# A chunked recurrence and two feed-forward layers on one core: how values are loaded, who copies the keys, and how the first layer's last two blocks are ordered

## The chip, the cores and the metric

The kernel runs on one NeuronCore of a Trainium2 chip. Its engines work side by side, each through its own queue in the order written: TensorE (PE, matmuls; PEld are its weight loads), VectorE (DVE), ScalarE (ACT), GpSimd (POOL), and SyncE (SP), whose queue here issues all DMA transfers to 16 DMA engines. The metric is the device time of one execution, in microseconds.

## The reference

Three steps follow each other. For 4 x 8 heads and 768 steps a state of 40 x 40 is read, decayed and updated; then two feed-forward layers work on 3072 tokens of 320 values, 2048 wide inside.

```python
for t in range(S):
    y[:, :, t] = np.einsum('bhd,bhde->bhe', rt, state)
    Sa = np.einsum('bhde,bhe->bhd', state, at)
    state_decay = state * wt[:, :, None, :] - np.einsum('bhd,bhe->bhde', Sa, bt)
    state = state_decay + np.einsum('bhd,bhe->bhde', vt, kt)
...
h = x @ w_in                                       # layer one
g = np.where(pos, h, np.where(neg, 0.0, (h + beta) ** 2 / (4.0 * beta)))
x = g @ w_out
...
h = x @ w_in                                       # layer two
r = np.maximum(h, 0.0)
g = s * (r * r) + b
return g @ w_out
```

The weights arrive as 64-bit floats.

## The kernel before

**Attention.** The 768 steps are cut into 24 chunks of 32 steps; two chunks make a unit (NU = 12). Per unit, `prep_a` builds running products of the decays, scales keys and a, and forms a triangular matrix, which `inverse` and `mend` invert. Per chunk, `chain_a` carries the state: xp, then up, then sp (the new state, from xr and the keys in kbi), and `chain_b` gives the output: tq (the state turned, copied into kbs), tp (copied into the upper half of vu), gg (from vu and ggr), py (from ggr and kbs). So the keys stand twice in SBUF: in KBI, written by DVE from tk and tb in `keys`, and in KBS, copied from KBI. Values lie in VU, whose lower half is loaded per chunk by `loads_v`, and whose upper half takes tp.

**Layers.** Layer one works on blocks of 256 tokens (12 of them, two chunks each), layer two on blocks of 512 (6). `fin0` and `fin1` make h for two slices or one slice of 128 inner columns, `post` turns h into g and splits it into a high part gh (ACT) and a rest gl (POOL in layer one, DVE in layer two), `fout0` and `fout1` add its product with w_out into acc. Output products run two steps behind the input products (LAG = 2). Every product is made of three, high by high, high by low and low by high, in float32r. `tok_tile` turns a tile of tokens with PE (ptx) and splits it likewise; layer one's input tiles have two slots (xh), so block n takes the slot of block n-2.

**Weights.** Each of 16 slices has two parts (w_in, 384 words a partition, and w_out, 320). `loads_w` brings the 64-bit words, `convert` makes 32-bit floats of them (ACT L233 and L234, DVE L235 and L236, POOL L238: t) and `split` a high part (L326) and the rest (L327). A slice of layer two lies where layer one's slice lay: its load waits until the last block of layer one has used that slice (`fin`, `fout`).

**Order.** The instructions are not put in this order by hand: `Order` is a list scheduler that runs when the program is built. Each function above is a thread that yields operations with planned durations, waits on flags, takes slots and sets its urgency (`Prio`, from START, STEP, TILE and DUE). At each step the engine that can begin earliest takes the most urgent of its operations ready within a small window. Filler matmuls (`warm`, L1022) keep PE busy until the first two input tiles of layer one are there. Planned durations set only the order; on the chip each queue waits for its semaphores.

## Time and profile before

| what | value |
|---|---|
| median of 3 runs | 1259.22 us (1254.14 to 1263.78) |
| the profiled execution | 1254.48 us, its span 1252.7 us |
| PE, PE weight loads | 1127.8 us, 1018.9 us |
| DVE, ACT, POOL | 730.4 us, 738.4 us, 343.4 us |
| mean granted clock of PE | 0.945 |
| DMA, first queue | 164054 packets, 124.69 MB, 40.7% of 16 engines' span |

Busy times overlap, and each is a share of the whole span. The stages differ: the first 150 us fill the pipeline, then attention and layer one share the engines to about 770 us, then layer one goes on alone to 861 us, and layer two takes the rest. The granted clock is 1 at 2.4 GHz and 0.5 at 1.2 GHz; a mean lies between.

### The profile page before, as it was taken

Reading aid. Unit: us, or ns where it says so; the run is one execution under the profiler, and the core shown is the slowest. Engines: PE = TensorE matmul, PEld = TensorE weight load, DVE = VectorE, ACT = ScalarE, POOL = GpSimd, SP = SyncE. Lnnn points to the kernel's source line nnn. Section 1 sums busy time; section 2 is a strip of 40 time slices with the busy share of each in tenths; the row PEclk is TensorE's granted clock in tenths of the full one; section 3 lists DMA queues with packets and bytes.
Section 4 is the critical chain, followed back from the end, with each engine's and each line's share of the span. In section 5 each row is a group of like instructions: output and inputs, shape, how many; then the busy total and the mean of one; then the engine's idle time right before and its main releaser. Section 6 shows DMA issues by size and latency. Waiting matters only on the chain. (4 is left out here: it accounts for less than half of the span.)

```text
span 1252.7 us, 45743 instructions
## 1 busy us (share of the span) xinstructions
PE 1127.8 (90%) x19834; PEld 1018.9 (81%) x19834; DVE 730.4 (58%) x1629; ACT 738.4 (59%) x1521; POOL 343.4 (27%) x299
## 2 busy tenths in 40 slices
PE   4798787898999889897999999998989999999995
PEld 4797776787888778776887899998878989888895
DVE  4777886636866776665786443237974344444432
ACT  2434774465675556655565576779876555555552
POOL 4456572321552323414141112335420000000000
PEclk9898698888999999889898999999989999999998
DMA  7875646545558657565644231129001010101001
GB/s 201 255 213 157 145 89 160 131 99 125 150 110 168 132 128 165 138 154 127 153 97 99 53 99 39 36 66 349 14 1 47 1 47 1 47 7 28 17 6 24
DMA packets 164264, 127.71 MB, mean 102 GB/s; under 512 B 118838, under 2 KB 137398, under 8 KB 162806
## 3 DMA queue, kind: packets, MB, share of 16 engines
q1 hardware_dynamic: 164054, 124.69, 40.7%
q8 instruction: 158, 2.59, 0.9%
q14 instruction: 52, 0.43, 0.1%
HBM read 90.83 MB, written 19.66 MB: 88 GB/s over the span
## 5 line engine op out<-in xcount | busy, mean ns | idle before, releaser
L926 POOL TENSOR_TENSOR gl<-g,gh 128x512 fp32r<-128x512 f32 x96 | 126.1, 1314 | 450.2 <-ACT gh L924 377.7
L946 PE MATMUL h<-xh,w 128*128 128x256 f32 x1152 | 234.5, 306 | 5.1 <-DVE g L914 3.5
L946 PEld LDWEIGHTS h<-xh,w 128*128 128x128 f32 x1152 | 186.4, 202 | 12.3 <-DVE g L914 4.0
L973 PE MATMUL acc<-w,gh 128*128 128x320 f32 x768 | 187.4, 330 | 2.0 <-issue 2.0
L991 PE MATMUL acc<-w,gh 128*128 128x320 f32 x768 | 174.6, 314 | 1.2 <-DVE o L1002 0.8
L924 ACT CAST gh<-g 128x512 fp32r<-128x512 f32 x192 | 118.8, 619 | 70.9 <-DVE g L914 40.8
L991 PEld LDWEIGHTS acc<-w,gh 128*128 128x128 f32 x768 | 133.6, 191 | 10.4 <-ACT o L1004 1.5
L926 DVE TENSOR_TENSOR gl<-g,gh 128x512 fp32r<-128x512 f32 x96 | 71.6, 746 | 116.1 <-ACT gh L924 114.4
L973 PEld LDWEIGHTS acc<-w,gh 128*128 128x128 f32 x768 | 127.2, 193 | 7.9 <-issue 1.7
L973 PE MATMUL acc<-w,gl 128*128 128x320 f32 x384 | 120.8, 315 | 1.8 <-issue 1.6
L914 DVE SCALAR_TENSOR_TENSOR g<-h,g 128x512 f32<-128x512 f32 x96 | 65.9, 686 | 96.2 <-ACT h L913 84.0
L991 PE MATMUL acc<-w,gl 128*128 128x320 f32 x384 | 120.1, 313 | 1.8 <-DVE gl L926 1.7
L946 PE MATMUL h<-xl,w 128*128 128x256 f32 x384 | 113.2, 295 | 3.0 <-issue 3.0
L920 ACT ACTIVATE g<-g,sbt 128x512 f32<-128x512 f32 x96 | 78.4, 817 | 60.3 <-DVE g L918 60.2
L911 ACT ACTIVATE g<-h,sbt 128x512 f32<-128x512 f32 x96 | 66.0, 688 | 64.8 <-PE h L946 59.2
L918 DVE SCALAR_TENSOR_TENSOR g<-h,g 128x512 f32<-128x512 f32 x96 | 66.3, 690 | 61.8 <-ACT g L917 61.7
L917 ACT ACTIVATE g<-h 128x512 f32<-128x512 f32 x96 | 57.4, 598 | 71.2 <-PE h L956 71.2
L1022 PE MATMUL h<-w 128*128 128x256 f32 x616 | 84.6, 299 | 16.4 <-ACT w L326 16.4
L1022 PEld LDWEIGHTS h<-w 128*128 128x128 f32 x616 | 80.6, 205 | 17.7 <-ACT w L326 16.4
L238 POOL TENSOR_TENSOR t<-t,w 128x384 int32<-128x384 int32 x64 | 68.0, 1070 | 92.2 <-DVE t L236 74.0
L956 PE MATMUL h<-xx,w 128*128 128x512 f32 x288 | 77.9, 405 | 4.6 <-ACT w L326 2.8
L946 PEld LDWEIGHTS h<-xl,w 128*128 128x128 f32 x384 | 77.8, 203 | 3.3 <-issue 3.2
(103 smaller groups left out, 2192.8 us busy)
## 6 DMA issues: line engine op xcount, KB each, us to landing
w<-in_w_in SPq DMA_DIRECT2D x32, 384.0 KB
w<-in_w_out SPq DMA_DIRECT2D x32, 320.0 KB
ekb<-in_kb_em SPq DMA_DIRECT2D x12, 832.0 KB
vu<-in_v_em SPq DMA_DIRECT2D x24, 416.0 KB
ggr<-in_r_em SPq DMA_DIRECT2D x24, 416.0 KB
kbs<-kbi SPq DMA_DIRECT2D x48, 160.0 KB
tk<-ekb SPq DMA_DIRECT2D x48, 128.0 KB
suf<-in_ws_em SPq DMA_DIRECT2D x12, 429.0 KB
```

What stands on the lines that cost most here:

```text
L238: (pool, n, lambda: nc.gpsimd.tensor_tensor(out=t, in0=t, in1=lo, op=ALU.add)),
L911: yield act(512, lambda: nc.scalar.activation(out=g, in_=h, func=AF.Relu, bias=sbt[:, 2:3]), more=93)
L914: yield dve(512, lambda: nc.vector.scalar_tensor_tensor(out=g, in0=h, scalar=1.0, in1=g, op0=ALU.subtract, op1=ALU.add))
L918: yield dve(512, lambda: nc.vector.scalar_tensor_tensor(out=g, in0=h, scalar=0.0, in1=g, op0=ALU.max, op1=ALU.mult))
L920: yield act(512, lambda: nc.scalar.activation(out=g, in_=g, func=AF.Identity, scale=sbt[:, 0:1], bias=sbt[:, 1:2]), more=230)
L924: yield act(512, lambda: nc.scalar.copy(out=gh, in_=g))
L926: yield mk(512, lambda: eng.tensor_tensor(out=gl, in0=g, in1=gh.bitcast(F32), op=ALU.subtract))
L946: yield pe(8 * 118, lambda: [nc.tensor.matmul(h[:, i, :], lhsT=a, rhs=b, start=m == 0, stop=m == 7) for m, (a, b) in enumerate(mm)])
L956: yield pe(4 * 224, lambda: [nc.tensor.matmul(h, lhsT=a, rhs=b, start=4 * i + m == 0, stop=4 * i + m == 7) for m, (a, b) in enumerate(mm[4 ...
L973: yield pe(6 * 147, lambda: [nc.tensor.matmul(acc[0, n][u], lhsT=a, rhs=b, start=p == 0 and m == 0, stop=p == NFF // 2 - 1 and m == 5) for ...
L991: yield pe(3 * 147, lambda: [nc.tensor.matmul(acc[1, n][u], lhsT=a, rhs=b, start=f == 0 and m == 0, stop=f == NFF - 1 and m == 2) for m, ( ...
L1022: yield pe(2 * 109, lambda: [nc.tensor.matmul(h[:, i, :], lhsT=wh[:, 0:128], rhs=wh[:, 0:256], start=True, stop=True) for i in range(2)], ...
```

## The change

Four edits. The values of a chunk are loaded without the zeros of the upper half, as two DMAs of 40 partitions with runs of 128 B instead of one of 104 partitions with rows of 4096 B; VU is cleared once by POOL. KBS gets its second copy of the keys from two ACT copies instead of two DMAs. In layer one, blocks 10 and 11 are worked off together, slice by slice, and begin when both have their input; block 11's accumulators take the slots of py and a. In layer two, the high part of the weights is made by POOL (a cast, `tensor_copy`) instead of ACT, and loads and conversions of its weights are due one unit earlier.

```diff
@@ -309,7 +309,7 @@
         yield Op("POOL", 500, lambda: nc.gpsimd.memset(LN, 0.0))
         yield pool(1, lambda: nc.gpsimd.memset(ones, 1.0))
         yield pool(1, lambda: nc.gpsimd.memset(tot, 0.0))
-        for i, t in enumerate(XA + XR + [KBS]):
+        for i, t in enumerate(XA + [VU] + XR + [KBS]):
             yield Op("POOL", 890, lambda t=t: nc.gpsimd.memset(t, 0.0))
             if i < 4:
                 od.set("clearx", i + 1)
@@ -321,9 +321,12 @@
     def hold(f, part, dtype):
         return wts.tile([128, 2 * (DM if part else 384)], dtype, tag=f"w{f}_{part}", name="w")
 
-    def split(w, t, n, mk, eng):
+    def split(l, w, t, n, mk, eng):
         wh, wl = w[:, 0:n], w[:, n:2 * n]
-        yield act(n, lambda: nc.scalar.copy(out=wh, in_=t.bitcast(F32)))
+        if l:
+            yield pool(n, lambda: nc.gpsimd.tensor_copy(out=wh, in_=t.bitcast(F32)), rate=1.2)
+        else:
+            yield act(n, lambda: nc.scalar.copy(out=wh, in_=t.bitcast(F32)))
         yield mk(n, lambda: eng.tensor_tensor(out=wl, in0=t.bitcast(F32), in1=wh.bitcast(F32), op=ALU.subtract))
 
     raw = [{}, {}]
@@ -331,10 +334,10 @@
     def loads_w(l):
 
         for f in range(NFF):
-            yield Prio(START + DUE["weights"] + TILE * f - 30 + (STEP * (NU - 1) + 60) * l)
+            yield Prio(START + DUE["weights"] + TILE * f - 30 + (STEP * (NU - 2) + 60) * l)
             for part in range(2):
                 if l:
-                    yield Wait(("fout" if part else "fin", (NBLK - 1) * NFF // 2 + f // 2 + 1))
+                    yield Wait(("fout" if part else "fin", (NBLK - 1) * NFF // 2 + f // 2 + 1), (("xr0", NC)))
                 elif f:
                     yield Wait((f"cl0{part}", f))
                 n = DM if part else 384
@@ -346,7 +349,7 @@
 
         n = DM if part else 384
         for f in range(odd, NFF, 2):
-            yield Prio(START + DUE["weights"] + TILE * f + (STEP * (NU - 1) + 60) * l)
+            yield Prio(START + DUE["weights"] + TILE * f + (STEP * (NU - 2) + 60) * l)
             yield Wait((f"cl{l}{part}", f + 1))
             w = raw[l].pop((f, part))
             yield Acq(f"t{part}")
@@ -354,7 +357,7 @@
             for mk, size, op in f64_ops(nc, w.rearrange("p (n x) -> p n x", x=2), t, n):
                 yield mk(size, op)
             w = hold(f, part, F32R)
-            yield from split(w, t, n, *((dve2, nc.vector) if l else (pool, nc.gpsimd)))
+            yield from split(l, w, t, n, *((dve2, nc.vector) if l else (pool, nc.gpsimd)))
             wtile[l][f, part] = (w[:, 0:n], w[:, n:2 * n])
             od.set(f"w{l}{part},{f}")
             od.rel(f"t{part}")
@@ -656,7 +659,9 @@
             if i:
                 od.rel("tk")
             yield Wait(("Y", c))
-            yield dma(128 * 2560, lambda: [nc.sync.dma_start(out=KBS[r0:r0 + 64, x], in_=KBI[r0:r0 + 64, x]) for x, r0 in ((0, 64), (1, 0))], 2, ("kbs", c + 1), 650)
+            for x, r0 in ((0, 64), (1, 0)):
+                yield act(640, lambda: nc.scalar.copy(out=KBS[r0:r0 + 64, x], in_=KBI[r0:r0 + 64, x]), x > 0)
+            od.set("kbs", c + 1)
 
     def decays():
         for c in range(NC):
@@ -679,8 +684,9 @@
     def loads_v():
         for c in range(NC):
             yield due("chain", c / 2)
-            yield Wait(("lk", 1), ("G", c))
-            yield dma(104 * 4096, lambda: nc.sync.dma_start(out=VU.rearrange("p a x t -> p (a x t)"), in_=v_em[c]), 1, ("ldv", c + 1))
+            yield Wait(("clear", 1), ("G", c))
+            yield dma(80 * 2048, lambda: [nc.sync.dma_start(out=VU[64 * x:64 * x + 40, :, 0, :], in_=v_em[c, x].rearrange("e (p t) -> e p t", t=C))
+                                          for x in range(2)], 2, ("ldv", c + 1))
 
     def loads_r():
         for c in range(NC):
@@ -964,16 +970,20 @@
     def fout0(n, p):
         yield Wait((f"g0,{n},{p}", 1), (f"w01,{2 * p}", 1), (f"w01,{2 * p + 1}", 1))
         gh, gl = gs.pop((0, n, p))
+        where = ("py", "a") if n == NBLK - 1 else ("o0", "o1")
         if p == 0:
-            for u in range(2):
-                yield Acq(f"o{u}")
-            acc[0, n] = [po.tile([128, DM], F32, tag=f"o{u}", name="acc") for u in range(2)]
+            for slot in where:
+                yield Acq(slot)
+            if n == NBLK - 1:
+                acc[0, n] = [pa.tile([128, DM], F32, tag="y", name="acc", bufs=1), pa.tile([128, DM], F32, tag="a", name="acc")]
+            else:
+                acc[0, n] = [po.tile([128, DM], F32, tag=f"o{u}", name="acc") for u in range(2)]
         for u in range(2):
             mm = [x for i in range(2) for x in g_products(0, gh, gl, 2 * p + i, 256 * i + 128 * u)]
             yield pe(6 * 147, lambda: [nc.tensor.matmul(acc[0, n][u], lhsT=a, rhs=b, start=p == 0 and m == 0, stop=p == NFF // 2 - 1 and m == 5)
                                        for m, (a, b) in enumerate(mm)])
             if p == NFF // 2 - 1:
-                od.spawn(finish(0, n, u, f"o{u}"), due("moe", n).value)
+                od.spawn(finish(0, n, u, where[u]), due("moe", n).value)
         od.rel("gh")
         od.set("fout", n * NFF // 2 + p + 1)
 
@@ -1026,20 +1036,21 @@
         late = []
         yield Wait(("const", 1))
         for l in range(2):
-            for n in range(NBLK // 2 if l else NBLK):
-                yield due("moe", 2 * n + NU if l else n)
-                yield Wait((f"xr{l}", 4 * n + 4 if l else 2 * n + 2))
+            for ns in [(n,) for n in range(NBLK // 2)] if l else [(n,) for n in range(NBLK - 2)] + [(NBLK - 2, NBLK - 1)]:
+                yield due("moe", 2 * ns[0] + NU if l else ns[0])
+                yield Wait((f"xr{l}", 4 * ns[0] + 4 if l else 2 * ns[-1] + 2))
                 steps = NFF if l else NFF // 2
                 for p in range(steps):
-                    yield from (fin1 if l else fin0)(n, p)
-                    late.append((fout1 if l else fout0, n, p))
-                    if p == steps - 1:
-                        for slot in (("tk", "tk", "ew") if n % 2 else ("ekb", "es")) if l else ("xh",):
-                            od.rel(slot)
-                        od.set(f"blk{l}", n + 1)
-                    if len(late) > LAG:
-                        fout, *at = late.pop(0)
-                        yield from fout(*at)
+                    for n in ns:
+                        yield from (fin1 if l else fin0)(n, p)
+                        late.append((fout1 if l else fout0, n, p))
+                        if p == steps - 1:
+                            for slot in (("tk", "tk", "ew") if n % 2 else ("ekb", "es")) if l else ("xh",):
+                                od.rel(slot)
+                            od.set(f"blk{l}", n + 1)
+                        if len(late) > LAG:
+                            fout, *at = late.pop(0)
+                            yield from fout(*at)
         for fout, *at in late:
             yield from fout(*at)
 
@@ -1185,7 +1196,7 @@
     d["ws_em"], d["wp_em"] = units(e[..., 1:]), units(e[..., :C])
     d["kb_em"] = units(np.stack([emaj(x["k"]), emaj(x["b"])], axis=2))
     d["a_em"] = np.ascontiguousarray(x["a"].reshape(NP, 2, NC, C, D).transpose(2, 1, 4, 0, 3)).reshape(NC, 2, D, NP * C)
-    d["v_em"] = emaj(x["v"], 0, 0, C).reshape(NC, 104, -1)
+    d["v_em"] = np.ascontiguousarray(x["v"].reshape(NP, 2, NC, C, D).transpose(2, 1, 4, 0, 3)).reshape(NC, 2, D, NP * C)
     e = emaj(x["r"])
     d["r_em"] = np.zeros((NC, 104, 2, NP, C), f)
     d["r_em"][:, 0:40, 0], d["r_em"][:, 64:104, 1] = e[:, 0:40], e[:, 64:104]
```

What this does to the order, at three places. Line numbers of the new file are 3 to 11 higher from the second edit on.

First, SP's queue in the attention stage. Before, one stretch of it:

```order
L569 DMA lscr_172<-ln 64x512 x2
L683 DMA vu<-in_v_em 104x1024
L587 DMA lt<-lscr_172 128x8x32
L406 DMA ekb<-in_kb_em 104x2048
L477 DMA ascr_161<-am 128x8x32
L659 DMA kbs<-kbi 64x640 x2
L689 DMA ggr<-in_r_em 104x1024
L400 DMA pre<-in_wp_em 104x1024
```

After, the same stretch:

```order
L572 DMA lscr_172<-ln 64x512 x2
L480 DMA ascr_161<-am 128x8x32
L590 DMA lt<-lscr_172 128x8x32
L480 DMA ascr_161<-am 128x8x32
L409 DMA ekb<-in_kb_em 104x2048
L556 DMA la<-ascr_161 64x16x16 x2
L403 DMA pre<-in_wp_em 104x1024
```

And ACT's queue after, at one chunk of that stage (xr, kbs, x and gh are written here):

```order
L917 ACTIVATE g<-h,sbt 128x512
L918 ACTIVATE h<-g,sbt 128x512
L919 ACTIVATE h<-h 128x512
L729 COPY xr_103<-up 32x320 x3
L663 COPY kbs<-kbi 64x640 x2
L729 COPY xr_103<-up 32x320
L930 CAST gh<-g 128x512
L790 COPY kbs<-tq 40x320 x2
L897 COPY x<-x 128x64
```

The loads of kbs are gone from SP, and two copies to kbs stand on ACT, here between the third and the last copy to xr.

Second, PE's queue where block 10 begins (acc are block 9's output products, ptx turns an input tile, h the next input products). Before:

```order
L973 MATMUL acc<-w,gh 128x320 x2
L973 MATMUL acc<-w,gl 128x320
L973 MATMUL acc<-w,gh 128x320 x2
L973 MATMUL acc<-w,gl 128x320
L865 MATMUL ptx<-ident,x 128x128 x3
L973 MATMUL acc<-w,gh 128x320 x2
L973 MATMUL acc<-w,gl 128x320
L973 MATMUL acc<-w,gh 128x320 x2
L973 MATMUL acc<-w,gl 128x320
L946 MATMUL h<-xh,w 128x256
L946 MATMUL h<-xl,w 128x256
```

After:

```order
L983 MATMUL acc<-w,gh 128x320 x2
L983 MATMUL acc<-w,gl 128x320
L983 MATMUL acc<-w,gh 128x320 x2
L983 MATMUL acc<-w,gl 128x320
L871 MATMUL ptx<-ident,x 128x128 x3
L983 MATMUL acc<-w,gh 128x320 x2
L983 MATMUL acc<-w,gl 128x320
L983 MATMUL acc<-w,gh 128x320 x2
L983 MATMUL acc<-w,gl 128x320
L871 MATMUL ptx<-ident,x 128x128 x3
L952 MATMUL h<-xh,w 128x256
L952 MATMUL h<-xl,w 128x256
```

Both times the ptx turns tiles of block 11, whose slot block 9 has just given back. Before, block 10's h needs none of them, and its own input lies ready. After, the first h belongs to the pair, for which both tiles must be split, and the second ptx stands directly ahead of it.

Third, DVE's queue where layer two's first gl stands (g and gl are the blocks' activations, t and w the weights' conversion). Before:

```order
L236 SCALAR_TENSOR_TENSOR t<-w,t 128x320
L236 SCALAR_TENSOR_TENSOR t<-w,t 128x384
L918 SCALAR_TENSOR_TENSOR g<-h,g 128x512
L871 TENSOR_TENSOR xl<-ptx,xh 128x2x128
L872 TENSOR_TENSOR xd<-ptx,xd 64x128
L918 SCALAR_TENSOR_TENSOR g<-h,g 128x512
L926 TENSOR_TENSOR gl<-g,gh 128x512
L327 TENSOR_TENSOR w<-t,w 128x320
L327 TENSOR_TENSOR w<-t,w 128x384
L327 TENSOR_TENSOR w<-t,w 128x320
L327 TENSOR_TENSOR w<-t,w 128x384
L926 TENSOR_TENSOR gl<-g,gh 128x512
```

After:

```order
L920 SCALAR_TENSOR_TENSOR g<-h,g 128x512
L330 TENSOR_TENSOR w<-t,w 128x384
L924 SCALAR_TENSOR_TENSOR g<-h,g 128x512
L1012 COPY o<-acc 128x320
L330 TENSOR_TENSOR w<-t,w 128x320
L330 TENSOR_TENSOR w<-t,w 128x384
L932 TENSOR_TENSOR gl<-g,gh 128x512
L236 SCALAR_TENSOR_TENSOR t<-w,t 128x320
L924 SCALAR_TENSOR_TENSOR g<-h,g 128x512
L235 TENSOR_SCALAR t<-w 128x384
L235 TENSOR_SCALAR t<-w 128x320
L235 TENSOR_SCALAR t<-w 128x384
```

Before, four subtractions (w<-t,w) follow the first gl; after, three stand ahead of it. In the whole queue, 9 of the 32 L235, 9 of the 32 L236 and 5 of the 32 subtractions stood ahead of that gl before, and 14, 13 and 13 now.

## Rows read from the trace of the kernel before

**Rows 1.** By stage: from:to, length, busy PE PEld DVE ACT POOL, PE clock, DMA share, GB/s.

```profile
150.00:765.90 615.90, 550.28 (x14799) 488.85 (x14793) 397.16 (x1020) 367.69 (x820) 195.96 (x160) 0.93 0.55 122
765.90:799.80 33.90, 33.90 (x423) 33.07 (x420) 9.13 (x21) 23.91 (x45) 10.32 (x8) 1.00 0.14 40
799.80:861.30 61.50, 61.50 (x475) 61.24 (x473) 25.73 (x52) 50.55 (x101) 25.35 (x21) 1.00 0.42 141
861.30:938.30 77.00, 67.28 (x326) 57.46 (x325) 67.74 (x116) 62.55 (x133) 30.39 (x29) 0.91 0.21 75
938.30:997.40 59.10, 59.10 (x334) 53.25 (x333) 25.72 (x42) 34.69 (x59) 0.00 (x0) 1.00 0.10 25
```

**Rows 2.** PE's waits, 150 to 766 us: total us, times, longest.

```profile
PE pq L607 <- issue: 11.3, 7, 4.6
PE tq L762 <- issue: 10.2, 4, 5.2
...
PE sp L741 <- ACT vu L802: 1.3, 2, 0.8
...
PE pl L596 <- issue: 0.7, 1, 0.7
```

**Rows 3.** PE in order of time near 708 us: start, length, group.

```profile
707.75 0.57 PE L607 MATMUL pq<-pn,en 32*16 32x16 f32 x50
709.52 0.27 PE L607 MATMUL pq<-pn,en 32*16 32x16 f32 x14 [1.21 <-issue]
```

**Rows 4.** Busy time in the first and last of seven long gaps.

```profile
209.49:214.74 5.25, 0.00 (x1) 0.00 (x0) 3.54 (x12) 0.32 (x1) 0.69 (x1) 0.85 0.88 202
...
617.39:620.35 2.96, 0.00 (x1) 0.03 (x1) 0.11 (x1) 0.06 (x1) 0.00 (x0) 0.84 0.91 202
```

**Rows 5.** PE's waits, 861 to 939 us.

```profile
PE ptx L865 <- DMA x<-x2scr: 2.4, 1, 2.4
```

**Rows 6.** Busy time while one load of vu, of aa, two of kbs move.

```profile
747.00:749.60 2.60, 2.60 (x79) 2.43 (x78) 1.58 (x4) 1.75 (x5) 0.00 (x0) 1.00 0.66 170
690.50:691.60 1.10, 1.01 (x29) 0.71 (x27) 1.05 (x4) 0.45 (x1) 0.00 (x0) 1.00 0.77 119
241.90:244.60 2.70, 0.95 (x77) 0.81 (x80) 2.51 (x14) 1.01 (x3) 0.00 (x0) 0.87 0.70 138
```

**Rows 7.** Instructions by line: a GpSimd memset.

```profile
L313 POOL MEMSET kbs<- 128x1280 f32 x1 | 1.2, 1170 | 0.0
```

**Rows 8.** SP's queue, waits ahead of the kbs loads.

```profile
SPq L659 <- PE py L832: 30.8, 16, 12.1
...
SPq L659 <- PE ptx L865: 19.9, 3, 18.5
```

**Rows 9.** Instructions by line: two ACT copies of other sizes.

```profile
L784 ACT COPY kbs<-tq 40x320 f32<-40x320 f32 x92 | 38.6, 420 | 27.0 <-PE tq L762 25.9
...
L499 ACT ACTIVATE tk<-suf 104x1024 f32<-104x1024 f32 x12 | 12.7, 1061 | 0.2
```

**Rows 10.** PE in order of time near 146 us.

```profile
146.31 0.87 PE L865 MATMUL ptx<-ident,x 128*128 128x128 f32 x3 [4.84 <-DVE x L884]
```

**Rows 11.** Instructions by line, 836 to 936 us: conversions and their neighbours.

```profile
L238 POOL TENSOR_TENSOR t<-t,w 128x384 int32<-128x384 int32 (+1 forms) x32 | 33.6, 1058 | 42.9 <-DVE t L236 24.9 <-ACT g L920 5.4 <-DVE t L235 3.5
...
L236 DVE SCALAR_TENSOR_TENSOR t<-w,t 128x384 int32<-128x384 int32 (+1 forms) x32 | 21.0, 671 | 0.2
...
L327 DVE TENSOR_TENSOR w<-t,w 128x384 fp32r<-128x384 f32 (+1 forms) x32 | 18.4, 597 | 1.9 <-ACT w L326 1.8
...
L926 DVE TENSOR_TENSOR gl<-g,gh 128x512 fp32r<-128x512 f32 x15 | 15.5, 1031 | 1.7 <-ACT gh L924 1.6
L326 ACT CAST w<-t 128x384 fp32r<-128x384 f32 (+1 forms) x32 | 15.3, 482 | 2.3 <-POOL t L238 2.1
L235 DVE TENSOR_SCALAR t<-w 128x384 int32<-128x384 int32 (+1 forms) x32 | 14.6, 475 | 0.1
...
L914 DVE SCALAR_TENSOR_TENSOR g<-h,g 128x512 f32<-128x512 f32 x8 | 5.5, 688 | 11.4 <-ACT h L913 10.0 <-POOL t L238 1.5
```

## Prediction

> **What bounds the kernel now.** I read the page's shares of busy time first (TensorE, PE, leads), then the busy time by stage [rows 1], then PE's waits in the stages where it isn't full. The stages are: start to 150.0 us (first chunks, filler matmuls); 150.0 to 765.9 us (the attention chain, with blocks 0 to 8 of layer one between its steps); 765.9 to 861.3 us (blocks 9 to 11 of layer one, PE full); 861.3 to 938.3 us (block 0 of layer two); then five more blocks, of 59.1 us for the second. Two stages leave something to win.
>
> In the attention stage PE is busy 550.3 of 615.9 us at a mean granted clock of 0.93, and no compute engine is full (DVE 397.2, ACT 367.7) [rows 1]. What PE waits for there is mostly "issue": nine rows, from 11.3 down to 0.7 us, make 43.2 us, while the largest wait for ACT is 1.3 us [rows 2]. Such a gap can fall in the middle of one uninterrupted group: 50 of the 64 matmuls of pq run, PE stands for 1.21 us, then the other 14 follow [rows 3]. No operand can arrive between two halves of one group, so I read it as instructions arriving late. In the seven longest gaps (2.7 to 5.3 us, 24.0 us in all) the DMA engines are 0.50 to 0.96 busy, 0.78 weighted by length, against 0.55 over the stage [rows 1, 4]. So the stage is PE work plus stalls that come when DMA piles up, plus the lower of PE's two clock levels (1.2 instead of 2.4 GHz) in part of it.
>
> Block 0 of layer two takes 77.0 us against 59.1 for block 1: 17.9 us too much [rows 1]. DVE is busy 67.7 us of it (88%), ACT 62.6; the weights of layer two are being converted there. PE also waits 2.4 us for one x load, behind weight loads on SP [rows 5].
>
> **Values: smaller loads.** One load of 104 rows of 4096 B kept the DMA engines 0.66 busy for 2.60 us: 0.66 x 2.60 x 16 = 27.5 us of engine time. The new form moves 2 x 40 x 16 = 1280 runs of 128 B. A load of 1024 such runs, aa, kept them 0.77 busy for 1.10 us: 13.6 us, so 17.0 for 1280 [rows 6]. Saved: 10.5 us a chunk. The upper half of vu, now zeros from DRAM, needs one more GpSimd memset at the start: about 1.0 us, by the 1170 ns of a 1280-element one [rows 7].
>
> The Trainium skill (Perfetto Trace Analysis, DMA Optimizations) speaks against this: transfers under 2 KB have significant overhead, and it advises larger ones. The trace bears it out by the byte (131 KB in 13.6 us of engine time against 426 KB in 27.5), but a chunk now moves 164 KB instead of 426. If the rule ate the whole saving, 26 instead of 36.5 us a chunk would go (below), and the sum would be 4 us worse.
>
> **Keys' second copy: from a DMA to ACT.** The two loads of kbs kept the engines 0.70 busy for 2.70 us, 30.2 us, of which some 86% (320 of 373 KB) is theirs: 26 us [rows 6]. Together 36.5 us a chunk less, for the 22 chunks of the stage 803 of 0.55 x 16 x 615.9 = 5420 us: 15% less time of the DMA engines. SP loses the kbs issues, which waited 30.8 us for py and 19.9 us for ptx with later loads queued behind them [rows 8].
>
> If the stalls shrink with the traffic, 43.2 us lose 6.5; since they stand where DMA piles up, I take 20%, 8.6 us. The low clock costs 0.07 x 615.9 = 43 us [rows 1]; only part of it follows these stalls, so I take 15% of half, 3.2 us. Sum -12, bounds 0 (stalls by instructions alone) and -30 (half the stalls, a fifth of the clock).
>
> The cost: two ACT copies of 64x640 a chunk. Between 0.42 us (320 elements) and 1.06 (1024) [rows 9] the line gives 0.71 each, 31 us in the stage: ACT goes from 60 to 65%. PE waits for ACT almost nowhere now [rows 2], so I take +1; the bound is +31, if every copy stands ahead of a chain copy. The order shows two directly ahead of the last xr copy, for which sp waits. Behind them on ACT's queue stand the chain's copies and the blocks' activations.
>
> **The start.** In the new order 670 filler matmuls stand ahead of block 0 where 614 stood, and one more pl and pq. Before, PE stood 4.84 us there for the x of chunk 1 [rows 10]; filler covers that now. What follows ptx is longer (28 filler matmuls and two small groups): +2 us, from -3 (the gap is covered) to +7 (it stays, and the groups come on top).
>
> **The last two blocks together.** PE's work is the same. Three things change. (1) A weight tile becomes free when both blocks have used it, over the whole pair instead of in the last block, so loads and conversions get 61.5 us (799.8 to 861.3) [rows 1] instead of the last half of it. (2) The pair starts only when both its inputs are there, and block 11's slot of xh is free only after block 9's last product. By the order, ptx of chunk 23 now stands directly ahead of the pair's first product: a transpose, an ACT cast and a DVE subtraction must end first, and no product stands between to cover them. I take +1.5 (0 to +3). (3) Accumulators of block 11 come from py and a, free by then: nothing.
>
> In block 0 of layer two, by the order, 14, 13 and 13 of the 32 passes L235, L236 and of the subtractions precede the first gl, where 9, 9 and 5 did. Taken from DVE there: 5 x 0.475 + 4 x 0.671 + 8 x 0.597 = 9.9 us [rows 11]. ACT loses its casts there, 27 x 0.482 = 13 us, and stops mattering.
>
> **GpSimd's cast.** Some 18 of 32 fall into block 0. No row has this operation: the nearest are a memset (1170 ns for 1280, so 0.35 for 384) and a two-input add (1.058) [rows 7, 11]. I take 0.5, one input being nearer to the memset. It isn't free for DVE: gl on DVE, between GpSimd's adds, takes 1.031 us on average against 0.688 for an operation of the same size that reads PSUM [rows 11], so DVE waits while GpSimd runs. I add 3 us: 67.7 - 9.9 + 3 = 60.8 us of DVE; at today's 88% the block takes 69, at 95% 64. I take 67: -10 (0 to -17.9). The x loads that PE waited for stand between fewer weight loads; that is inside the 10.
>
> In the pair ACT gets the conversions. Its 50.5 us there now hold 9 of them and 5 casts by the order, 9 x 2 x 0.482 + 5 x 0.482 = 11 us if a pass is as long as a cast [rows 1, 11]; without them 39.5, with 14 x 2 x 0.482 = 13.5 on top 53 of 61.5 us. That is tight: +2 (0 to +8).
>
> **Sum.** -12 + 1 + 2 + 1.5 - 10 + 2 = -15.5 from the profiled execution's 1254.5 us (span 1252.7 and 1.8 around it): 1239. That execution is 4.7 us below the median of the three runs, 1259.2, so against the median: 1244.
>
> **Rivals.** (A) The stalls stay, because they are set by PE's own instruction stream: small instructions pass faster than the next ones come. For it: the gaps stand in groups of tiny matmuls (pq, tq, py) [rows 2]. Against: the DMA share in the gaps [rows 4]. Then -12 falls away: 1256. The Trainium skill (Runtime: NRT & Kernel Launch, Instruction fetch mechanics) says fetching is mostly hidden; by that rule the DMA's share would gain nothing either, 1256. The split group [rows 3] speaks against it.
>
> (B) Slower: the wait for py moves with the copy. On SP the kbs issues waited 50.7 us for PE [rows 8]; now ACT waits, and with it the activations of the blocks and the chain's copies. If two thirds reach PE, +34: 1278. It decides as soon as PE's waits for ACT in the attention stage grow from some 2 us to over 15.
>
> (C) GpSimd's cast is as slow as its add. Then 32 x 1.06 = 34 us more of GpSimd between 800 and 930, in which DVE's two-input passes stand. The Trainium skill (SBUF — State Buffer, Who interferes with whom) calls that an exclusive lock; the mean of gl agrees. Block 0 gains nothing and the pair loses 6: 1244 + 10 + 4 = 1258.
>
> (D) The stalls halve: -30 for -12: 1226.
>
> **Chances.** Forecast 0.50, A 0.19, B 0.12, C 0.11, D 0.08. A measurement of this kernel tells about 1% (12.6 us; the three runs span 9.6) from no change, so faster means under 1246.6. Of the forecast's 0.50 some 0.42 lie there, 0.06 of A and C (both end at 1256 to 1258, with the same spread), 0.08 of D: 0.56; I give 0.54. B and a bad end of the rest: slower 0.12. The range from 1227 to 1265 leaves out B, half of D and the ends of the others.
>
> **What the changed profile would show.** Right: in the attention stage issue waits of 30 to 38 us, DMA share near 0.47, PE's waits for ACT under 5 us; the block after layer one's end 64 to 70 us long; the cast near 0.5 us. Wrong: issue waits at 43 us or more with less DMA (A); ACT idle before the kbs copies for py, PE behind it (B); a cast of 1 us, DVE's subtractions over 0.8 us on average (C). The prediction fails on size if clock and stalls move by chance with the new order: 20 us of low clock more or less would hide all the rest.

## The result, and the profile after

The changed kernel takes 1244.34 us (median of four runs, 1238.59 to 1254.19) where the kernel before takes 1258.18; the ratio is 0.9898, 95% interval 0.9855 to 0.9941. The profiled execution took 1240.35 us, its span 1238.6. Medians are over all executions, ratios over those within 1.5% of the fastest of their kernel. The total lies near the forecast, but by stage the gain came from other places than the sum said.

The windows by stage, with the same columns as [rows 1]: the start, the attention stage, block 9, the pair, block 0 of layer two.

```profile
0.00:168.00 168.00, 124.82 (x2340) 117.61 (x2341) 116.14 (x249) 67.71 (x161) 87.18 (x91) 0.89 0.69 177
168.00:763.60 595.60, 538.91 (x14666) 480.73 (x14664) 387.20 (x989) 390.45 (x848) 187.09 (x153) 0.95 0.48 103
763.60:798.30 34.70, 34.32 (x428) 33.17 (x423) 9.63 (x22) 25.41 (x48) 10.33 (x8) 1.00 0.11 32
798.30:860.00 61.70, 60.85 (x464) 60.34 (x465) 41.19 (x66) 50.28 (x100) 37.36 (x37) 1.00 0.49 164
860.00:924.80 64.80, 60.44 (x332) 53.09 (x331) 57.44 (x101) 49.12 (x97) 36.15 (x44) 1.00 0.20 65
```

The attention stage is 20.3 us shorter than in [rows 1] (595.6 for 615.9), but it starts 17.9 us later (168.0 for 150.1), and layer one ends at 860.0 for 861.3: up to there almost nothing is won. Block 0 of layer two is 12.2 us shorter (64.8 for 77.0): 4.4 us of idle PE instead of 9.7, and 60.4 us of PE's own work instead of 67.3, at a clock of 1.00 instead of 0.91. The DMA share of the attention stage fell from 0.55 to 0.48, as forecast.

PE's waits in the attention stage (as [rows 2]; "issue" is a wait for which the profile shows nothing that ended it):

```profile
PE up L724 <- issue: 12.8, 5, 4.4
PE acc L983 <- issue: 9.4, 4, 5.3
PE tq L768 <- issue: 8.2, 7, 2.1
PE xp L709 <- issue: 3.1, 2, 2.1
...
PE pl L599 <- DMA lt<-lscr: 0.8, 1, 0.8
...
PE xp L709 <- ACT pn L603: 0.4, 1, 0.4
```

All ten issue rows sum to 40.9 us, against 43.2 before; 30 to 38 was forecast. For ACT PE waits 0.4 us, so the ACT copies hold PE up nowhere that the profile shows. One of them takes what the line through [rows 9] gave, 0.72 us, and ACT waited 8.9 us for py ahead of them:

```profile
L663 ACT COPY kbs<-kbi x48: 721/725/730, 38.2 to 763.7; 64x640 f32<-64x640 f32 x48
...
  PE py L838: 8.9, 14
```

PE in order of time at the start (as [rows 10]):

```profile
150.69 4.10 PE L1032 MATMUL h<-w 128*128 128x256 f32 x32
160.97 0.87 PE L871 MATMUL ptx<-ident,x 128*128 128x128 f32 x3 [6.19 <-DVE x L890]
161.50 4.09 PE L1032 MATMUL h<-w 128*128 128x256 f32 x20
```

The wait for chunk 1's x, which more filler was to cover, is still there: 6.19 us for 4.84 (3.34 in the second profile of this kernel, below). Instructions by line from 836 to 925 us (as [rows 11]):

```profile
L236 DVE SCALAR_TENSOR_TENSOR t<-w,t 128x320 int32<-128x320 int32 (+1 forms) x27 | 18.5, 693 | 0.0
L235 DVE TENSOR_SCALAR t<-w 128x384 int32<-128x384 int32 (+1 forms) x26 | 17.4, 691 | 1.3 <-ACT w L233 1.3
...
L330 DVE TENSOR_TENSOR w<-t,w 128x320 fp32r<-128x320 f32 (+1 forms) x27 | 16.1, 615 | 0.3 <-POOL w L327 0.3
L327 POOL CAST w<-t 128x320 fp32r<-128x320 f32 (+1 forms) x27 | 14.9, 556 | 1.1
```

The cast takes 0.56 us, near the 0.5 taken. DVE's one-input pass L235 went from 475 to 691 ns on average.

### The profile page after: what moved, and what is told of

The parts are those of the page before. It is cut to its first block, busy times and chain, and to the rows that moved or that the text cites. A ratio compares the mean times of both kernels' runs of the same rounds, so it can differ in the third digit from the quotient of the medians.

```text
span 1238.6 us, 45822 instructions
## 1 busy us (share of the span) xinstructions
PE 1118.9 (90%) x19890; PEld 1014.1 (82%) x19890; DVE 738.6 (60%) x1629; ACT 757.4 (61%) x1537; POOL 358.1 (29%) x332
## 3 DMA queue, kind: packets, MB, share of 16 engines
q8 instruction: 158, 2.59, 0.9%
## 4 chain that ended last, share of the span: by engine, by line
PE 67%; DVE 12%; issue 7%; ACT 5%; DMA 4%; SPq 2%; POOL 1%; DVEq 0%; ACTq 0%; POOLq 0%
PE h L962 12%; PE acc L1001 12%; PE h L952 12%; PE acc L983 11%; PE h L1032 5%; PE tq L768 2%; PE sp L747 2%; PE gg L817 2%; PE py L838 1%; PE ap L466 1%; PE up L724 1%; PE xp L709 1%; DVE xr L759 1%; PE tp L802 1%; DVE ln L570 1%
## 5 line engine op out<-in xcount | busy, mean ns | idle before, releaser
L932 POOL TENSOR_TENSOR gl<-g,gh 128x512 fp32r<-128x512 f32 x96 | 124.8, 1300 | 433.9 <-ACT gh L930 397.3
L952 PE MATMUL h<-xh,w 128*128 128x256 f32 x1152 | 223.5, 296 | 3.0 <-DVE xh L878 2.1
L952 PEld LDWEIGHTS h<-xh,w 128*128 128x128 f32 x1152 | 178.4, 193 | 9.2 <-DVE xh L878 2.3
L932 DVE TENSOR_TENSOR gl<-g,gh 128x512 fp32r<-128x512 f32 x96 | 68.1, 709 | 117.6 <-ACT gh L930 117.5
L920 DVE SCALAR_TENSOR_TENSOR g<-h,g 128x512 f32<-128x512 f32 x96 | 66.1, 689 | 89.0 <-ACT h L919 65.9
L952 PE MATMUL h<-xl,w 128*128 128x256 f32 x384 | 109.7, 286 | 0.0
L1032 PE MATMUL h<-w 128*128 128x256 f32 x672 | 94.6, 302 | 16.3 <-ACT w L329 16.3
L1032 PEld LDWEIGHTS h<-w 128*128 128x128 f32 x672 | 89.6, 208 | 17.8 <-ACT w L329 16.3
L962 PE MATMUL h<-xx,w 128*128 128x512 f32 x288 | 75.4, 395 | 2.5 <-DVE w L330 2.4
L983 PEld LDWEIGHTS acc<-w,gl 128*128 128x128 f32 x384 | 76.2, 198 | 0.5 <-issue 0.5
```

The lines of the kernel that those rows point to most:

```text
L920: yield dve(512, lambda: nc.vector.scalar_tensor_tensor(out=g, in0=h, scalar=1.0, in1=g, op0=ALU.subtract, op1=ALU.add))
L932: yield mk(512, lambda: eng.tensor_tensor(out=gl, in0=g, in1=gh.bitcast(F32), op=ALU.subtract))
L952: yield pe(8 * 118, lambda: [nc.tensor.matmul(h[:, i, :], lhsT=a, rhs=b, start=m == 0, stop=m == 7) for m, (a, b) in enumerate(mm)])
L962: yield pe(4 * 224, lambda: [nc.tensor.matmul(h, lhsT=a, rhs=b, start=4 * i + m == 0, stop=4 * i + m == 7) for m, (a, b) in enumerate(mm[4 ...
L983: yield pe(6 * 147, lambda: [nc.tensor.matmul(acc[0, n][u], lhsT=a, rhs=b, start=p == 0 and m == 0, stop=p == NFF // 2 - 1 and m == 5) for ...
L1032: yield pe(2 * 109, lambda: [nc.tensor.matmul(h[:, i, :], lhsT=wh[:, 0:128], rhs=wh[:, 0:256], start=True, stop=True) for i in range(2)], ...
```

## The experiments

The scheduler makes a new order from every edit, so an edit made alone also moves hundreds of other instructions. Most experiments therefore keep an order: the planned operation stays as it was, and only the instructions that it issues are exchanged. "In place" means that. Three groups of four kernels ran, each group beside runs of the kernel before on the same chip (medians 1258.1, 1263.0 and 1256.1 us); ratios are to those. The theory was that less DMA engine time means fewer late instructions on PE, and that pairing and cast shorten block 0 of layer two; the rivals were that PE's own stream sets the stalls, that SP's waits for py were what hurt, and that order and clock move by chance.

**Both attention edits in place, old order.**

```diff
-yield dma(128 * 2560, lambda: [nc.sync.dma_start(out=KBS[r0:r0 + 64, x], in_=KBI[r0:r0 + 64, x]) for x, r0 in ((0, 64), (1, 0))], 2, ("kbs", c + 1), 650)
+yield dma(128 * 2560, lambda: [nc.scalar.copy(out=KBS[r0:r0 + 64, x], in_=KBI[r0:r0 + 64, x]) for x, r0 in ((0, 64), (1, 0))], 2, ("kbs", c + 1), 650)
-yield dma(104 * 4096, lambda: nc.sync.dma_start(out=VU.rearrange("p a x t -> p (a x t)"), in_=v_em[c]), 1, ("ldv", c + 1))
+yield dma(104 * 4096, lambda: [c or nc.gpsimd.memset(VU, 0.0)] +
+          [nc.sync.dma_start(out=VU[64 * x:64 * x + 40, :, 0, :], in_=v_em[c, x].rearrange("e (p t) -> e p t", t=C))
+           for x in range(2)], 1, ("ldv", c + 1))
```

> The kernel before, in its own order, with the smaller value loads and the two ACT copies put exactly where the old loads stood; every other instruction keeps its place. The forecast's theory (stalls follow the DMA traffic): DMA share of the attention stage from 0.55 to about 0.48, PE's issue waits there from 43 to about 35 us, time 8 to 12 us below the kernel before. Rival A (PE's own instruction stream sets the stalls): issue waits stay at 40 us or more, time within 3 us of before. Rival B (ACT waits for py with the copies): PE's waits for ACT in the stage above 15 us, time 10 us or more above.

Measured: 1242.46 us, ratio 0.9895 (0.9867 to 0.9922), some 13 us less. The attention stage and the rest of layer one, and PE's waits in the former:

```profile
148.30:751.50 603.20, 541.03 (x14796) 480.89 (x14793) 393.74 (x1020) 394.67 (x860) 195.59 (x160) 0.95 0.49 105
751.50:846.80 95.30, 95.30 (x894) 94.21 (x892) 34.79 (x73) 74.98 (x146) 35.63 (x29) 1.00 0.30 100
```

```profile
PE pl L596 <- DVE xr L755: 8.4, 4, 3.8
PE pq L607 <- issue: 8.2, 6, 4.5
...
PE tq L764 <- issue: 4.4, 5, 1.7
```

The issue rows sum to 30.2 us (43.2 before), layer one ends at 846.8 us (861.3). Two edits do alone what four do together. PE's waits for ACT rose from 2.7 to 7.2 us and those for DVE from 11.4 to 19.6: a part of rival B, smaller than the gain. So most of the 13 us of issue waits that are gone came back as other waits: in the stage PE is idle 62.2 us for 65.6, but busy 541.0 for 550.3 with the same matmuls, at a clock of 0.95 for 0.93. Averaged over its runs the granted clock is 0.953 against 0.942 for before on that chip.

**Each of the two alone**, by the same edits.

> The kernel before, in its own order, with the smaller value loads alone in the place of the old ones. Theory that DMA engine time is the cause: by my estimates values are 10.5 of the 36.5 us a chunk that both edits save, so 4 to 5 of the 15.6 us that both gave together: 1253 to 1254. Rival that SP's waits for py are the cause (they leave with the keys' copy alone): 1258, no change within 2 us.

> The kernel before, in its own order, with the keys' second copy alone made by ACT in the place of the DMAs. Theory of DMA engine time: 26 of 36.5 us a chunk, so 10 to 12 us less: 1246 to 1248. Rival that SP's waits for py are the cause: nearly all of the 15.6 us, 1242 to 1244. Rival B (ACT waits for py): above 1258.

Values alone: 1254.92 us, 0.9945 (0.9913 to 0.9978), about 7 us. Keys' copy alone: 1252.89, 0.9924 (0.9898 to 0.9950), about 10 us. Together 16 or 17, near the 13 of both. The values gained some 7 us where 4 to 5 were expected, a value that the interval still holds. They leave SP's wait for py in place (18.9 us in the profile, for 30.8) and give SP two loads to issue for one, and still gain; that speaks against SP as the cause. Issue waits don't show this gain: 52.4 us in the one profile of values alone. Nor, as far as one profile each can tell, does the gain follow DMA engine time in proportion. By the pages' shares (40.7% of 16 engines' span before, 40.0% with the values' edit, 37.8% with the keys') the values save some 100 us of it in all, 4 a chunk (7 a chunk where the keys' edit is made too, 37.5% for 37.8%), and the keys 580, 24 a chunk. 10.5 and 26 were forecast.

**The traffic put back, SP's wait not.** The old place on SP issues two DMAs of the same size, from KBI to unused DRAM instead of to KBS; ACT makes the copy.

```diff
+[(nc.scalar.copy(out=KBS[r0:r0 + 64, x], in_=KBI[r0:r0 + 64, x]),
+  nc.sync.dma_start(out=kbx[c][x], in_=KBI[r0:r0 + 64, x].rearrange("p a t -> p (a t)")))
+ for x, r0 in ((0, 64), (1, 0))]
```

> As the kernel with the keys' copy alone on ACT, in the order of before, but with two DMAs of the same size from KBI to unused DRAM in the old place on SP: the traffic is back, while SP no longer waits there for py. Theory of DMA engine time: near the kernel before, 1255 to 1260. Rival that SP's waits are the cause: within 3 us of the kernel with the copy alone on ACT.

Measured: 1262.69 us, 1.0014 (0.9977 to 1.0050): the gain is gone. Against the keys' copy alone, the difference is two transfers a chunk and their issues on SP, worth 10 to 11 us (0.8 to 0.9%). In the profile SP has no wait for py ahead of those two. The attention stage, first with the copy alone, then with the traffic back:

```profile
154.00:768.10 614.10, 552.56 (x14795) 490.97 (x14793) 395.14 (x1020) 394.69 (x860) 195.76 (x160) 0.93 0.50 112
```

```profile
155.00:772.30 617.30, 551.11 (x14795) 489.70 (x14792) 397.33 (x1020) 395.52 (x860) 195.81 (x160) 0.93 0.54 123
```

PE is idle 66.2 us there for 61.5. Issue waits are only 2.1 us of that (37.7 for 35.6); waits of pl for a load of lt are 3.0 (5.8 for 2.8), so part of the cost is a late operand.

**The old traffic in the new order.** The changed kernel with the old form of the value loads in place, and beside each ACT copy a DMA as above.

```diff
+yield act(640, lambda: (nc.scalar.copy(out=KBS[r0:r0 + 64, x], in_=KBI[r0:r0 + 64, x]),
+                        nc.sync.dma_start(out=kbx[c][x], in_=KBI[r0:r0 + 64, x].rearrange("p a t -> p (a t)"))), x > 0)
```

> The changed kernel in its own order, with the old form of the value loads, and beside ACT's two copies of the keys two DMAs of the same size from KBI to unused DRAM: the removed traffic is back, the order and the ACT work stay. The forecast's theory: DMA share of the attention stage back at 0.55 or above, issue waits 45 us or more, time 8 to 14 us above the changed kernel (1252 to 1258). Rival A: issue waits within 3 us of the changed kernel's 41, time within 3 us of it.

Measured: 1252.89 us, 0.9972 (0.9943 to 1.0000), so 8 to 10 us above the changed kernel, as expected. The expected signs in the trace did not come: the DMA share of the stage was 0.52, not 0.55, and issue waits were 35.0 us, less than the changed kernel's 40.9. What is worse there is the clock, 0.93 for 0.95 in the attention stage and 0.86 for 0.89 ahead of it:

```profile
0.00:170.00 170.00, 130.84 (x2341) 122.93 (x2341) 114.71 (x248) 67.48 (x161) 85.20 (x90) 0.86 0.70 185
170.00:777.70 607.70, 547.68 (x14667) 488.62 (x14665) 388.89 (x990) 390.57 (x848) 188.68 (x154) 0.93 0.52 121
```

**Pairing, due times and cast, old attention.** The changed kernel with the old lines of both attention edits.

> The changed kernel with the old value loads and the old DMA copy of the keys: pairing, due times and GpSimd's cast alone, in the order that the scheduler then makes. The forecast's theory (two halves of about equal worth): 1250 to 1256, first block of layer two 64 to 68 us, issue waits of the attention stage 43 us or more. The rival that the second half is the whole gain: 1244 to 1248, the same as the changed kernel within 3 us. The rival that the clock and the order by chance are the gain: anywhere from 1240 to 1262, with the granted clock explaining it.

Measured: 1252.75 us, 0.9938 (0.9895 to 0.9981), 5 to 8 us less than before, in the range expected. Issue waits were 37.9 us, not the 43 or more expected with the old traffic. Block 0 of layer two, within the 64 to 68 us expected:

```profile
861.60:929.30 67.70, 61.81 (x328) 53.96 (x328) 57.09 (x100) 48.95 (x96) 36.30 (x44) 0.97 0.19 59
```

**The cast alone, old order.**

```diff
-yield act(n, lambda: nc.scalar.copy(out=wh, in_=t.bitcast(F32)))
+yield act(n, lambda: (nc.gpsimd.tensor_copy if l else nc.scalar.copy)(out=wh, in_=t.bitcast(F32)))
```

> The kernel before, in its own order, with layer two's casts issued to GpSimd where ACT had them; nothing else changes. The forecast's theory (DVE sets the first block of layer two, the pair is what relieves it): the block stays at 74 to 80 us, time within 4 us of before, a cast 0.5 us. The rival that the cast alone gives the gain (ACT was the engine that held the conversions back): block 65 to 69 us, time 8 to 12 us below. Rival C (slow cast, port): block over 82 us, time 6 us or more above.

Measured: 1263.06 us, 1.0048 (1.0015 to 1.0082): slower by some 6 us (2 to 10), where less than 4 either way was expected. A cast took 0.65 us on average. The end of layer one, and block 0 of layer two:

```profile
770.10:867.20 97.10, 95.60 (x893) 94.22 (x892) 35.38 (x70) 74.09 (x142) 38.53 (x34) 1.00 0.33 108
867.20:943.60 76.40, 65.44 (x327) 55.85 (x326) 70.88 (x119) 51.92 (x103) 47.56 (x56) 0.93 0.20 69
```

The block hardly changed (76.4 for 77.0), as expected, although ACT lost 10.6 us in it: ACT does not set it. That DVE does, 70.9 us busy and so 3.1 more, fits but has no run of its own. The profile shows 1.7 us at the end of layer one (97.1 for 95.4); where the rest of the 2 to 10 us lies is open, since the code ahead is the same.

**All four edits, the attention part in place.** The kernel with pairing, due times and cast, and in it the first diff above.

> All four edits, but the two of the attention stage put in place: the order is the one that the scheduler makes for pairing, due times and cast alone, and the smaller value loads and ACT's copies stand where the old loads stood. If the two halves add up (15.6 us by the attention edits in the old order, 5.4 us by the other half): 1236 to 1239, below the changed kernel's 1244, with block 0 of layer one at about 150 us and layer one's end near 848 us. If the later start of block 0 in the changed kernel costs nothing: 1243 to 1246, like the changed kernel.

Measured: 1245.11 us, 0.9882 (0.9846 to 0.9918), about the changed kernel's ratio; layer one ends at 859.4 us, not near the 848 that a full sum would give. The product of the two halves would be 0.983, 6 us less; with intervals of 0.003 and 0.004 to either side of the halves that may be chance. The profile has 32.9 us of issue waits, but the attention stage at a clock of 0.93.

```profile
150.50:762.00 611.50, 549.02 (x14795) 488.38 (x14793) 392.65 (x1020) 394.32 (x860) 194.72 (x160) 0.93 0.49 104
859.40:928.30 68.90, 62.99 (x328) 55.11 (x327) 56.97 (x100) 48.93 (x96) 36.25 (x44) 0.95 0.19 58
```

**The changed kernel again, and its start.** The last group holds the changed kernel itself and one with a planned number altered, which only moves the order:

```diff
-yield dma(80 * 2048, lambda: [...], 2, ("ldv", c + 1))
+yield dma(104 * 4096, lambda: [...], 1, ("ldv", c + 1))
```

> The changed kernel itself, unaltered, to stand on the same chip beside the next three and to narrow its interval: ratio to before 0.986 to 0.994. If the four runs shown so far were lucky in their clock (0.943 to 0.959): ratio above 0.994.

> The changed kernel with one planned number altered: the scheduler counts a value load as long as the old one (one issue, 104 rows of 4096 B), the instructions issued are those of the changed kernel. In the order this gives 592 filler matmuls ahead of block 0 instead of 670. Theory that the late start of block 0 (168 us instead of 150) comes from that planned cost and costs time: block 0 at 148 to 154 us, 5 to 13 us below the changed kernel on the same chip. Rival that the late start costs nothing, because the attention chain runs ahead meanwhile: within 3 us of the changed kernel.

The changed kernel: 1243.02 us, 0.9890 (0.9838 to 0.9943). The other: 1239.11 us, 0.9852 (0.9805 to 0.9899), between what the two theories said: 4 us less, with intervals that overlap, so no clear difference. Block 0 of layer one begins at 157.0 us instead of 171.5 (148 to 154 was expected), with 592 filler matmuls ahead of it instead of 670. The attention stage and block 0 of layer two of the changed kernel, then the attention stage of the other:

```profile
171.50:766.80 595.30, 538.28 (x14666) 480.26 (x14664) 388.40 (x989) 390.91 (x848) 187.33 (x153) 0.95 0.48 103
863.50:929.40 65.90, 61.23 (x330) 54.58 (x329) 57.54 (x101) 49.24 (x97) 36.16 (x44) 0.97 0.20 64
```

```profile
157.00:762.50 605.50, 546.07 (x14827) 483.93 (x14825) 400.43 (x1023) 396.30 (x865) 200.17 (x164) 0.95 0.49 105
```

The wait for chunk 1's x at the start of the changed kernel, in this profile:

```profile
164.61 0.87 PE L871 MATMUL ptx<-ident,x 128*128 128x128 f32 x3 [3.34 <-DVE x L890]
```

Of 14.5 us of earlier start, 4.3 are left at the end of the stage (762.5 for 766.8).

**The changed kernel with its cast on ACT again**, in place.

```diff
-yield pool(n, lambda: nc.gpsimd.tensor_copy(out=wh, in_=t.bitcast(F32)), rate=1.2)
+yield pool(n, lambda: nc.scalar.copy(out=wh, in_=t.bitcast(F32)), rate=1.2)
```

> The changed kernel in its own order, with layer two's casts issued to ACT again. Theory that the pair's earlier loads relieve DVE, and that the cast by GpSimd costs rather than gives (4 to 5 us slower when moved alone in the old order): 2 to 6 us below the changed kernel, block 0 of layer two 62 to 65 us. The forecast's view (without GpSimd ACT gets too tight in the pair): 3 to 8 us above, ACT busy 57 us or more of the 62 in the pair.

Measured: 1245.89 us, 0.9917 (0.9881 to 0.9954); beside the changed kernel's 0.9890 on that chip no clear difference, so neither of the two expectations came. Block 0 of layer two takes the same time, with DVE 3.2 us less busy and ACT 6.8 us more: in this order DVE's load does not set it. ACT in the pair was 54.5 of 62.7 us busy.

```profile
863.10:929.20 66.10, 61.37 (x331) 54.34 (x330) 54.33 (x101) 56.01 (x118) 24.56 (x23) 0.97 0.20 64
```

```profile
L235 DVE TENSOR_SCALAR t<-w 128x384 int32<-128x384 int32 (+1 forms) x26 | 15.4, 613 | 1.3 <-ACT w L233 1.3
L330 DVE TENSOR_TENSOR w<-t,w 128x320 fp32r<-128x320 f32 (+1 forms) x27 | 13.8, 525 | 0.6 <-ACT w L327 0.5
```

**Pairing and due times, attention in place, no cast.**

> Smaller value loads and ACT's copies in place, pairing and due times, but no cast by GpSimd; the order is the scheduler's for pairing and due times. If the cast costs in any order: ratio to before 0.984 or below, the fastest so far, block 0 of layer two 64 to 67 us. If the cast is needed to make room on ACT in the pair: ratio 0.989 or above, block 0 of layer two over 70 us or the pair over 66 us.

Measured: 1238.52 us, 0.9847 (0.9788 to 0.9907). With the altered planned number (0.9852) this is the fastest here; both lie below the changed kernel, neither by more than the intervals. Block 0 of layer two takes 70.5 us, and the last three blocks of layer one 98.1 (95.4 before). The block's length is the sign named for a cast that makes room on ACT, the ratio is near the one named for a cast that costs; neither theory is borne out whole.

```profile
749.80:847.90 98.10, 96.33 (x889) 93.55 (x885) 53.84 (x96) 82.65 (x168) 46.94 (x39) 1.00 0.35 114
847.90:918.40 70.50, 62.68 (x333) 55.29 (x332) 55.28 (x93) 53.41 (x110) 21.17 (x19) 0.95 0.19 60
```

**What ends an issue wait.** Without a run of its own: in the kernel before, PE waits from 209.49 to 214.74 us ([rows 4]) in the middle of tq's matmuls, and the DMA view of the stretches 209.49 to 212.0 and 212.0 to 213.4 us (queue, kind: packets, MB, share) has

```profile
q1 hardware_dynamic: 298, 0.52, 87.3%
...
q1 hardware_dynamic: 67, 0.28, 78.3%
q8 instruction: 1, 0.02, 5.5%
```

One 16 KB packet of instructions starts at 212.03, after PE has stood for 2.5 us, and ends at 213.26; PE goes on 1.48 us later. It recurs: in the fourteen profiles there are 360 issue waits of over 0.5 us between 100 us and the last three blocks of layer one, and 324 of them end 1.2 to 1.8 us after such a packet landed. Only 11% of all moments in those stretches lie so. The page of the changed kernel counts 158 of these packets, 2.59 MB, for 39,780 matmuls and weight loads.

## Why the prediction was right, and where its steps were not

**Views and bounds: right in the main.** The issue waits are late instructions by what the packets show: nine in ten of those over 0.5 us end at the same distance behind one; the split group [rows 3] had only suggested it. One reading was wrong. The second gap shown in [rows 4], 617.39 to 620.35 us, is no issue wait but a wait for a load, as PE in order of time and PE's waits of 150 to 766 us show:

```profile
620.35 1.05 PE L596 MATMUL pl<-lt,aa 32*32 32x16 f32 x64 [2.96 <-DMA lt<-lscr]
```

```profile
PE pl L596 <- DMA lt<-lscr: 5.9, 3, 3.0
```

So part of the time goes with loads that come late, for which the sum had no term; the other six gaps are issue waits. By the rule of the Trainium skill (Runtime: NRT & Kernel Launch, Instruction fetch mechanics), fetching is mostly hidden; under this DMA load issue waits are 30 to 52 us of the attention stage in the profiles. Rival A falls: the same compute instructions with and without two DMAs a chunk differ by 0.9%.

**The attention term: right in sum, mis-sized inside.** -12 + 1 was forecast, 13 us are measured in the old order (interval 10 to 17). The keys' copy, forecast as seven tenths of it, gave about 10, the values about 7. The stalls' share was too large and the clock's too small. I gave 8.6 of the 12 us to the stalls and 3.2 to the clock. In the old order's profiles PE's idle time in the stage fell by 3.4 us and PE's own work by 9.3 (above). Over all runs there the granted clock rose by 0.011, and within the runs of the kernel before, on each of three chips, 0.01 of clock goes with 7 to 10 us. So more than half of the gain comes with the clock; why less traffic raises it is not shown. The Trainium skill's advice against transfers under 2 KB (Perfetto Trace Analysis, DMA Optimizations) holds by the byte here: 131 KB in runs of 128 B took 13.6 us of engine time, 426 KB in rows of 4096 B 27.5. But the smaller loads still gain.

**The sign I named for it was too sharp.** Issue waits of 30 to 38 us were to tell right from wrong. The same code gave 40.9, 39.3 and 31.8 us in three profiles (the changed kernel twice, and with its cast on ACT, which comes later). One profile can't resolve 8 us there; the time over many runs and the mean clock can. Over the five profiles with all the old traffic issue waits are 35.0 to 43.2 us, 39 on average; over the seven with both lighter transfers 30.2 to 40.9, on average 34. So about 5 us went.

**The start: the step that failed.** "Filler covers that now" is wrong: of the 56 more filler matmuls 30 stand ahead of the same ptx, which still waits 6.19 us (3.34 in the second profile), and 26 behind it. They come on top of the work there: PE is busy 124.8 us ahead of block 0 for 115.5. The block starts 18 us late where +2 was taken. Most of it is not lost, since the chain goes on meanwhile: of 14.5 us, 4.3 were left at the stage's end. The planned length of the value load causes most of the shift; with the old one in the plan the median is 4 us lower, inside the bounds of -3 to +7 but not clear of noise.

**The pair: +3.5 forecast** (bubble and ACT). The last three blocks took 96.4 us for 95.4: +1.

**Block 0 of layer two: right in size, its cause half right.** 67 us was forecast, 64.8 and 65.9 measured, so -11 to -12 for -10. Conversions moved ahead by pairing and due times do most of it: with them the block takes 66.1 us without GpSimd's cast in the changed kernel's order and 70.5 in the order planned without it, and with the cast alone 76.4. The forecast put all 10 us on DVE; of the 12.2 measured, 5.4 are idle PE and 6.8 PE's own work at a higher clock, which had no term. The 3 us that I added to DVE for GpSimd's work are there (57.5 for 54.3). The cast on GpSimd is worth nothing measurable in the new order and costs 2 to 10 us in the old one. Rival C had the right sign there, with too large a price.

**Total.** -15.5 was forecast and -13.8 measured, which is in part luck. Start and attention were to give -9 together. In the two profiles of the changed kernel the attention stage ends 2.3 us earlier (763.6 for 765.9) and 0.9 later (766.8), though with the attention edits in the old order it ends 14.4 earlier (751.5). So in these single profiles the new order gives back most of the attention gain, and the late start explains only some 4 us of that. Pair and block 0, together 3 to 5 us better than forecast, hid a part.

**Open:** whether the two halves add up (with the attention edits in place they fall 6 us short of their product, within what the intervals allow), how far a new order moves the clock by itself, and why the values' edit gains 7 us with so little engine time saved.

## What to carry to other kernels

DMA traffic can cost an engine time though no operand is late: where waits without a releaser end at a fixed distance behind instruction packets, a transfer that can be left out, padding and second copies included, is worth a run. Judge it by the time: a stall that is gone can come back as a wait for another engine while the clock brings the gain. A list scheduler answers each edit with a new order, which moved medians here by 4 to 6 us, within the intervals; try an edit first with the instructions exchanged in their old places, and then look at what the planned costs do. Moving work to an idle engine is a gain only if the engine relieved was the late one and the helper doesn't slow it.

## What was not expected of the hardware

Issue waits of over 0.5 us end 1.2 to 1.8 us after a 16 KB instruction packet landed (324 of 360). The packet's own time hardly changes with the load (mean 1.16 us in the attention stage before, 1.12 after); that it waits for its turn behind data is argued, since the trace shows packets only once they move.

GpSimd's work slows DVE's conversions: in the same order, the two-input subtraction L330 takes 616 ns with the cast on GpSimd and 525 with it on ACT, and the one-input pass L235 705 and 613 ns. These means mix two cases. In the kernel before, where L235 takes 475 ns, 17 of its 32 passes have no GpSimd instruction beside them and take 0.33 us on average, the other 15 take 0.64; in the second profile of the changed kernel 3 take 0.32 us alone and 22 take 0.76 beside GpSimd.
